# Sparse attention and a mixture of expert attentions: from masked full scores to 256 laid-out keys per query block, with a planned order of all parts

## The chip, the cores and the metric

The kernel runs on one core of a Trainium2 chip. The metric is the device time of one execution in microseconds (us), lower is better. Every time in a profile view is of one execution taken by the hardware profiler.

## The reference

Two stages follow each other, for 4 batches of 768 positions, all in fp32.

```
# stage a: 8 heads of 64, blocks of 32 positions, 24 blocks
scores = scale * q @ k.T
mask = |blk_i - blk_j| <= 1 | blk_i in (0, 23) | blk_j in (0, 23)
mask |= the 3 sampled key blocks of each query block
attn = softmax(where(mask, scores, -1e9)); x = attn @ v      # heads side by side: 512 columns
# stage b: 4 experts of 64, each a causal attention over x
logits = x @ w_gate; the two largest per position, softmax over them -> w
ye = softmax(causal(scale * (x @ wq) @ (x @ wk).T)) @ (x @ wv) @ wo
out = sum of w * ye over the two chosen experts
```

A query of blocks 1 to 22 sees at most 8 key blocks of 32: three of its neighbourhood, the first and the last, and three sampled ones, which may coincide with others. Queries of blocks 0 and 23 see all 768 keys. The weights of queries and keys are scaled so that the experts' scores spread widely, so the maxima are needed.

## The kernel before

**Units.** The work comes in 24 units: per batch four pairs of heads (stage a) and two pairs of experts (stage b). A unit has a first part (operands and maxima, `first_part`, L662) and a second one (`back`, L694: scores, weighted values, denominators).

**Scores.** `scores` (L332) computes transposed scores, keys on partitions and queries in columns, of all 768 keys in stage a and of the causal ones in stage b. Each is the sum of two products of rounded operands (fp32r, L354 and L355): one of the rounded halves, and one of the halves with what the rounding left (`split_hi`, `split_lo`, L250 and L257). The block mask and the negated maxima are further rows of the contraction, so the sum in PSUM is already masked and shifted. ScalarE takes the exponentials (L359, L361).

**Maxima.** Since queries lie in columns there, the maxima come from a second set of score products, queries on partitions, in one rounded product (`maxima_a` L281, `maxima_b` L301), reduced by VectorE (L288, L296, L319) and brought to a row by a transpose and a DMA (`rows_to`, L269).

**Weighted values.** `weighted` (L386) multiplies exponentials and values in full fp32, the two members of a pair in two column tiles of 64 of the PE array (L397, `tile_position=(0, 64 * j)`). The exponentials' sums are added up by GpSimd and VectorE over key tiles (L375, L380), brought across partitions by one-hot products in column tiles of 32 (`denominators`, L413), inverted, and spread over partitions through DRAM (`spread`, L438). `scaled` (L449) splits the result into halves again.

**Experts.** `project_v` (L506) and `load_b` (L562) project x, three rounded products per piece; `project_o` (L591) does the output. They wait for all four pairs of heads of their batch.

**Order.** The parts stand on one line, measured in TensorE's time; some 360 numbers (`PRM`) give their places, and the parts are emitted in that order (L782). Each engine runs its instructions in the order of emission; the semaphores follow from the tiles' uses. Loads go through SP's queue.

Of the kernel before, what the change touches and what calls it, by code (L numbers as in the profile page):

```python
# [16 lines left out]
DRAM = bass.MemoryType.DRAM

# Places of the parts on the line that the order of emission follows; a suffix names the unit.
PRM = dict(  # L20
    LAT=13.1, LAT_a0=12.354, LAT_a1=14.661, LAT_a2=13.384, LAT_b0=17.761, LAT_la0=16.415, LAT_la2=12.42,
    LAT_lb0=13.078, LAT_u=14.078, LAT_v=13.582, LAT_z=24.018, T0=9.302, alag=4.6, alag_a0=4.4, alag_a1=4.0,
    alag_a3=4.708, alag_b1=5.56, alag_la1=4.12, alag_la2=5.967, alag_lb0=8.0, alag_u=4.82, alag_v=5.0,
    alag_w=6.266, alag_y=4.503, alag_z=10.7, c0=1.562, c1=3.8, c2=-0.048, denlag=1.0, denlag_a0=1.581,
    denlag_a1=0.805, denlag_a2=1.457, denlag_a3=0.629, denlag_b0=3.008, denlag_b1=0.834, denlag_f=0.71,
    denlag_la0=0.93, denlag_la1=0.928, denlag_la3=0.912, denlag_lb0=1.946, denlag_u=1.483, denlag_v=0.048,
    denlag_w=1.004, denlag_y=1.221, denlag_z=0.78, fmin=4.924, fmin_a0=1.802, fmin_a1=2.272, fmin_a2=6.216,
    fmin_a3=1.633, fmin_b0=4.822, fmin_b1=4.309, fmin_la1=3.34, fmin_la2=4.016, fmin_la3=4.167,
    fmin_lb0=4.313, fmin_u=4.949, fmin_v=5.643, fmin_w=4.786, fr=0.85, fr_a0=0.7, fr_a1=0.742, fr_a2=0.941,
    fr_b1=0.825, fr_la0=1.085, fr_la1=0.802, fr_v=1.38, fr_y=0.875, fr_z=0.287, glag=0.499, glag_a0=3.123,  # L30
    glag_la0=5.028, glag_v=3.776, half=0, half_a0=1, half_a1=1, half_a2=1, half_b0=0, half_b1=0, half_la0=1,
    half_la1=1, half_la2=0, half_u=1, half_v=0, half_y=1, half_z=1, hi1=0.3, hi1_a1=0.291, hi1_a2=0.053,
    hi1_b0=0.045, hi1_b1=0.224, hi1_f=0.2, hi1_la0=0.481, hi1_la1=0.303, hi1_la2=0.45, hi1_la3=0.409,
    hi1_lb0=0.328, hi1_u=0.332, hi1_v=0.01, ld=2, ld_a0=4, ld_a2=2, ld_b0=3, ld_b1=0, ld_la1=2, ld_lb0=0,
    ld_u=4, ld_w=4, ld_y=2, ld_z=2, lo0=0.132, lo0_a0=0.093, lo0_a1=0.004, lo0_b1=0.001, lo0_f=0.005,
    lo0_la0=0.038, lo0_la1=0.03, lo0_la2=0.136, lo0_la3=0.006, lo0_lb0=0.122, lo0_u=0.117, lo0_v=0.142,
    lo0_w=0.137, lo0_y=0.181, lo0_z=0.194, lo1=0.921, lo1_a0=1.124, lo1_a1=0.807, lo1_a3=0.631,
    lo1_b0=1.141, lo1_b1=0.913, lo1_f=0.497, lo1_la0=0.693, lo1_la1=0.953, lo1_la2=0.039, lo1_la3=1.074,
    lo1_u=0.28, lo1_v=1.246, lo1_y=1.038, lo1_z=0.847, lol=0.366, lol_a1=0.412, lol_a2=0.388, lol_b0=0.371,
    lol_b1=0.332, lol_la0=0.479, lol_la1=0.153, lol_la2=1.504, lol_la3=0.02, lol_u=0.56, lol_v=0.163,  # L40
    lol_w=0.397, lol_y=0.155, lol_z=0.184, mE=3.139, mE_a0=4.355, mE_la0=13.339, mF0=5.0, mF0_a0=6.412,
    mF0_la0=7.098, mQ0=1.448, mQ0_a0=6.073, mQ0_la0=7.051, mQ1=22.409, mQ1_a0=15.958, mQ1_la0=20.473,
    mQ1s=0.807, mQ1s_a0=0.026, mQ1s_la0=1.316, mV=2.0, mV_a0=9.376, mV_la0=8.188, mld=0.0, mld_a0=0.053,
    mld_la0=0.037, mrd=1, mrd_a0=1, mrd_a1=0, mrd_a3=0, mrd_la0=0, mrd_la2=0, mrd_la3=0, mrd_lb0=0, mrd_u=0,
    mrd_v=1, mrd_w=1, mrd_y=1, mrd_z=1, oB=0.794, oB_a0=0.738, oB_a1=0.485, oB_b1=0.351, oB_la0=1.25, pg=1,
    pg_a0=1, pg_a1=2, pg_a3=2, pg_b1=2, pg_f=2, pg_la1=1, pg_la2=2, pg_la3=2, pg_u=2, pg_v=2, pg_y=1,
    pg_z=2, pvs=1.69, pvs_a1=1.676, pvs_b0=1.635, pvs_b1=2.26, pvs_la1=1.8, pvs_la2=1.6, pvs_u=2.865,
    pvs_v=1.971, pvs_z=0.562, ql=-0.014, ql_a0=0.1, ql_a1=-0.0, ql_a3=-0.02, ql_b0=0.027, ql_b1=0.001,
    ql_la0=-0.005, ql_la2=-0.018, ql_la3=-0.04, ql_lb0=0.003, ql_u=-0.023, ql_v=0.011, ql_w=0.012,
    ql_y=-0.032, ql_z=0.02, row0=0.4, rowlag=3.325, rowlag_a0=2.927, rowlag_a2=3.319, rowlag_a3=1.938,  # L50
    rowlag_b0=3.085, rowlag_b1=4.446, rowlag_f=1.273, rowlag_la0=3.327, rowlag_la1=3.362, rowlag_la2=0.687,
    rowlag_lb0=1.967, rowlag_u=1.881, rowlag_v=2.19, rowlag_w=4.275, rowlag_y=2.969, rowlag_z=1.673,
    s1a=0.061, s1a_a1=0.163, s1a_a2=0.003, s1a_a3=0.123, s1a_b0=-0.0, s1a_b1=0.1, s1a_f=0.148, s1a_la1=0.07,
    s1a_la2=0.015, s1a_la3=0.1, s1a_lb0=0.063, s1a_u=0.0, s1a_w=0.204, s1a_y=0.103, s1a_z=0.07, s1b=0.9,
    s1b_a0=0.645, s1b_a1=0.953, s1b_a2=0.971, s1b_b0=0.912, s1b_b1=1.046, s1b_la1=0.951, s1b_lb0=0.904,
    s1b_u=0.86, s1b_v=0.019, s1b_w=0.727, s1b_y=1.0, slot=21.5, slot_a0=37.307, slot_a1=24.896,
    slot_a2=21.953, slot_a3=20.799, slot_b0=8.629, slot_b1=13.986, slot_la0=37.0, slot_la1=21.201,
    slot_la2=21.575, slot_la3=20.0, slot_lb0=18.0, slot_u=10.28, slot_v=6.588, slot_w=26.089, slot_y=25.015,
    slot_z=21.0, slotO=7.453, slotO_a0=8.961, slotO_a1=10.96, slotO_la0=9.856, span0=7.0, subk=1, subk_a0=0,
    subk_a1=1, subk_a2=0, subk_a3=1, subk_b1=0, subk_f=1, subk_la0=0, subk_la1=1, subk_la2=0, subk_la3=0,  # L60
    subk_lb0=0, subk_v=1, subk_w=0, subk_y=0, subk_z=1, subq=1, subq_a0=1, subq_a1=1, subq_a2=0, subq_a3=1,
    subq_b0=1, subq_b1=0, subq_f=1, subq_la1=1, subq_la2=1, subq_la3=1, subq_u=0, subq_v=1, subq_w=0,
    tV=-0.022, tX=7.6, tb0=14.0, tb0L=16.0, tb1=18.397, tb1L=15.332, tf0=3.897, tf1=13.3, tf1L=7.285,
    to=15.0, toL=31.0, tq=1.952, tqL=14.997, vlag=0.747, vlag_a0=0.188, vlag_a1=0.968, vlag_a2=0.558,
    vlag_a3=0.731, vlag_b0=0.703, vlag_b1=1.037, vlag_la0=0.602, vlag_la2=1.208, vlag_la3=1.313,
    vlag_lb0=0.626, vlag_u=0.66, vlag_v=0.168, vlag_w=1.396, vlag_z=0.857, w0=0.007, wsp=55.0, xoff=1.0,
    xoff_a3=2.0, xoff_f=2.37, xoff_la3=0.571,
)
# [9 lines left out]
def block_sparse_then_moe(ctx: ExitStack, tc: tile.TileContext, qT, kT, v, samp, wg, wq, wk, wv, wo, out):  # L78
# [19 lines left out]
    wk2 = ctx.enter_context(tc.tile_pool(name="wk2", bufs=2))
    sm = ctx.enter_context(tc.tile_pool(name="sm", bufs=3))
    ps_st = ctx.enter_context(tc.tile_pool(name="ps_st", bufs=3, space=PSUM))  # L100
    ps_pv = ctx.enter_context(tc.tile_pool(name="ps_pv", bufs=1, space=PSUM))
    ps_s1 = ctx.enter_context(tc.tile_pool(name="ps_s1", bufs=3, space=PSUM))
    dram = ctx.enter_context(tc.tile_pool(name="dram", bufs=3, space=DRAM))
# [5 lines left out]
    NS = 2  # L109
    QA = [ops.tile([128, 2, S], F32R, name=f"QA{i}") for i in range(NS)]  # L110
    QB = [ops.tile([128, 2, S], F32R, name=f"QB{i}") for i in range(NS)]
    KB = [ops.tile([128, 2, S], F32R, name=f"KB{i}") for i in range(NS)]
# [703 lines left out]
```

## Time and profile before

| what | value |
|---|---|
| device time, three runs | 774.3, 776.44, 778.53 us; median 776.44 |
| the profiled execution: first to last instruction (the page gives no time of its own around that span) | 774.1 us |
| DMA moved | 37.45 MB, mean 48 GB/s |
| VectorE, ScalarE, GpSimd busy | 70%, 57%, 50% of the span |
| longest wait group of an engine | ScalarE L359 for TensorE L355, 177.6 us in all |
| SP issues | about 290 DMAs, the record of one 0.3 to 0.6 us |

The page gives for each engine the time in which an instruction of it ran. A matmul's record holds its way through the array too, so two that follow each other overlap in the records; the distance between their starts tells what one costs. "PEld" are the weight loads that go before matmuls. A matmul whose operands are both full fp32 shows as two records. "SPq" rows are DMAs that SyncE issues. The idle time of an engine that is not the bottleneck costs nothing.

### The profile page before, as it was taken

The numbers are of one execution on the slowest core, as the hardware profiler recorded it, in microseconds if no ns is written. First come the engines' busy times: TensorE is split into PE (matmuls) and PEld (weight loads), VectorE is DVE, ScalarE is ACT, GpSimd is POOL, SyncE is SP. The second block draws the span as 40 slices with busy tenths as digits, with TensorE's granted clock in tenths as the row PEclk, the third lists the DMA queues.
The fourth block names the chain that finished last, engine by engine and source line by source line (L and its number), as shares of the span: only waits on it lengthen the run. The fifth ranks groups of instructions, "written<-read, shape, count | busy, mean of one in ns | idle before, by whom it ended". The sixth has DMA issues, their size and how long they took to land.

```text
span 774.1 us, 11317 instructions
## 1 busy us (share of the span) xinstructions
PE 751.7 (97%) x4167; PEld 468.2 (60%) x4167; DVE 540.6 (70%) x878; ACT 441.3 (57%) x731; POOL 385.3 (50%) x325
## 2 busy tenths in 40 slices
PE   4999999999999999999999999999999999999996
PEld 2655555766556556576655655657565655586565
DVE  8887887537878858555778886834776985564634
ACT  8765764374576655428367656644655765535552
POOL 6665853145446935306534892632565655513450
PEclk9999999999999999999999999999999999999999
DMA  7123310102021221100301212120120200010022
...
DMA packets 33904, 37.45 MB, mean 48 GB/s; under 512 B 10428, under 2 KB 23480, under 8 KB 33848
## 3 DMA queue, kind: packets, MB, share of 16 engines
...
q14 instruction: 23, 0.19, 0.1%
...
## 4 chain that ended last, share of the span: by engine, by line
PE 89%; DVE 8%; issue 1%; ACT 1%; DMA 0%; ACTq 0%; DVEq 0%
PE pv L397 28%; PE st L354 13%; PE st L355 10%; PE st L575 9%; PE s L286 7%; PE s L311 5%; PE s L516 5%; PE s L601 4%; PE s L294 3%; PE s L413 3%; PE s L314 2%; DVE mx L288 2%; DVE sum L380 2%; DVE nm L298 1%; DVE u L457 1%
## 5 line engine op out<-in xcount | busy, mean ns | idle before, releaser
L359 ACT ACTIVATE pt<-st 128x512 f32<-128x512 f32 (+1 forms) x256 | 142.9, 582 | 182.3 <-PE st L355 177.6
L397 PE MATMUL pv<-pt,vr 128*64 128x256 f32 (+1 forms) x768 | 191.0, 499 | 0.0
L354 PE MATMUL st<-QA,KA 128*128 128x512 f32 (+4 forms) x512 | 176.8, 357 | 0.0
L355 PE MATMUL st<-QB,KB 128*128 128x256 f32 (+2 forms) x512 | 165.6, 338 | 0.0
L380 POOL TENSOR_TENSOR sum<-sum,pt 128x768 f32<-128x768 f32 (+2 forms) x88 | 141.0, 1604 | 29.8 <-ACT pt L361 25.2
L288 DVE TENSOR_REDUCE mx<-s 128x1 f32<-128x512 f32 x192 | 126.7, 681 | 28.6 <-PE s L286 27.4
L380 DVE TENSOR_TENSOR sum<-sum,pt 128x768 f32<-128x768 f32 (+3 forms) x104 | 101.1, 978 | 48.9 <-ACT pt L361 35.5
L266 POOL TENSOR_TENSOR QB<-qr,QB 64x768 fp32r<-64x768 f32 x32 | 62.5, 1955 | 133.6 <-ACT QB L264 122.8
L354 PEld LDWEIGHTS st<-QA,KA 128*128 128x128 f32 (+1 forms) x512 | 97.4, 190 | 38.1 <-issue 21.8
L397 PEld LDWEIGHTS pv<-pt,vr 128*64 128x64 f32 x768 | 58.6, 136 | 77.0 <-issue 61.6
L355 PEld LDWEIGHTS st<-QB,KB 128*128 128x128 f32 x512 | 97.7, 191 | 9.0 <-issue 1.1
L375 POOL TENSOR_TENSOR sum<-pt 128x768 f32<-128x768 f32 x32 | 61.0, 1917 | 83.3 <-PE s L413 33.2
L319 DVE TENSOR_REDUCE mx<-s 128x1 f32<-128x512 f32 (+3 forms) x128 | 59.5, 501 | 52.5 <-PE s L314 39.1
L361 ACT ACTIVATE pt<-st 128x512 f32<-128x512 f32 x128 | 75.5, 593 | 23.6 <-PE st L355 20.6
L286 PE MATMUL s<-KA,QA 128*128 128x512 f32 x192 | 79.6, 447 | 7.6 <-ACT KA L255 6.3
L366 POOL TENSOR_SCALAR_AFFINE_SELECT pt<-pt 128x128 f32<-128x128 f32 x96 | 36.1, 386 | 89.0 <-ACT pt L359 83.9
L296 DVE TENSOR_REDUCE mx<-s 128x2 f32<-128x512 f32 x96 | 65.5, 682 | 14.6 <-PE s L294 14.3
L397 PE MATMUL pv<-pt,vb 128*64 128x256 f32 (+3 forms) x320 | 62.9, 405 | 0.0
L286 PEld LDWEIGHTS s<-KA,QA 128*128 128x128 f32 x192 | 35.0, 195 | 40.2 <-DVE mx L288 8.5
L311 PE MATMUL s<-KA,QA 64*128 64x512 f32 (+3 forms) x128 | 50.0, 407 | 0.1
L294 PEld LDWEIGHTS s<-KA,QA 128*128 128x128 f32 x192 | 34.0, 196 | 20.8 <-DVE mx L288 11.1
L575 PE MATMUL st<-xh,wqkh 128*128 128x512 f32 (+1 forms) x128 | 45.1, 352 | 0.0
(140 smaller groups left out, 1096.4 us busy)
## 6 DMA issues: line engine op xcount, KB each, us to landing
...
rd<-rc SPq DMA_DIRECT2D x92, 1.5 KB
...
```

Of the source, the lines that this page charges most:

```text
L266: sub.tensor_tensor(dst[64 - o:128 - o, j], x, f(dst)[o:o + 64, j], op=ALU.subtract)
L286: nc.tensor.matmul(s, qa[:, j, r * 128:(r + 1) * 128], ka[:, j, 0:512], start=True, stop=True)
L288: nc.vector.tensor_reduce(mx[:, 0, j, r:r + 1], s, AX.X, op=ALU.max, negate=True)
L296: nc.vector.tensor_reduce(mx[:, 1, j, r - 1:r + 1], s, AX.X, op=ALU.max, negate=True)
L311: nc.tensor.matmul(s[:, o:o + n], qa[0:64, j, r * 128:(r + 1) * 128], ka[0:64, j, k0:k0 + n], start=True, stop=True)
L354: nc.tensor.matmul(s[:, o:o + n], ka[0:hi, j, kc], qa[0:hi, j, q0:q0 + n], start=True, stop=False)
L355: nc.tensor.matmul(s[:, o:o + n], kb_[:, j, kc], qb[:, j, q0:q0 + n], start=False, stop=True)
L359: nc.scalar.activation(p[:, t - t2, q0:q0 + n], s[:, 0:n], AF.Exp, scale=scale)
L361: nc.scalar.activation(p[:, :, q0:q0 + n], s.rearrange("p (a b) -> p a b", a=2), AF.Exp, scale=scale)
L380: eng.tensor_tensor(s_[:, q0:S], s_[:, q0:S], p[:, t - t2, q0:S], op=ALU.add)
L397: nc.tensor.matmul(pv[c][64 * j:64 * j + 64, a - c0:cw], vs(t, j), res["p"][t, j][:, a:a + w], start=t == 0, stop=t == last, tile_position ...
L575: nc.tensor.matmul(s[:, 0:cw], w[:, k, e * 2 * D:(e + 1) * 2 * D], a[:, k, c0:c0 + cw], start=n == 0, stop=n == 3 * KT - 1)
```

## The change

The whole body is new; inputs, outputs and the launch stay.

**Attention.** The unit is now two neighbouring query blocks (64 queries) of all 8 heads: 11 units per batch for blocks 1 to 22, and one for blocks 0 and 23 together (`ends`). GpSimd lays the 256 keys that each block may see side by side (`gather`: 96 of the neighbourhood, 64 of the first and last block, 96 sampled; block numbers in registers). SP loads the values in the same order from DRAM, a DMA for each sampled block (`values`; 7 DMAs per unit, of which 6 have a register address). Scores are full fp32 products of 64 rows by 32 columns, eight tiles of the PE array, queries on partitions; a bf16 product of a one-hot row with a mask row adds the mask for blocks that would count twice. So the maximum is one reduce along the row, the exponential takes it as a bias and returns its sum, and the denominator needs no product. The exponentials are transposed by TensorE (8 per unit), copied out of PSUM by ScalarE or VectorE, and weighted with the values in column tiles of 32 (32 products of 64 columns). x is scaled, transposed and split into rounded halves.

**Experts.** `experts` works on a batch in three chunks of two 128-query tiles, as x becomes ready. Scores (`rows`) are full fp32 products in two row halves of the array (64x128), one expert of a pair in each, over keys 0 to the diagonal; then the same steps: mask by a bf16 product, reduce, exponential with bias and sum, transposes, copies, weighting (128-column weights, 64 moving columns), scaling by gate and denominator, transpose, split, output product and store. The projections are the same three rounded products.

**Buffers.** K and Q of a batch have one buffer each, the laid-out keys and the values three each, x one.

**Order.** `Plan.run` replaces the numbers: each part has an engine, a duration, dependencies, buffers and a due time; a simulation of five engines, eight PSUM banks and buffer slots takes on each engine the ready part with the earliest due time, on TensorE with a preference for staying in the same tiling. The parts are emitted by their planned start. The experts' due times lie about one unit behind the last unit they need.

The core of the diff, after the removal of everything described above:

```diff
-        nc.tensor.matmul(s[:, o:o + n], ka[0:hi, j, kc], qa[0:hi, j, q0:q0 + n], start=True, stop=False)
-        nc.tensor.matmul(s[:, o:o + n], kb_[:, j, kc], qb[:, j, q0:q0 + n], start=False, stop=True)
...
+    def attention(b, u):
...
+        def gather(o):
+            pol.tensor_copy(K[:, :, :, 0:96], win)
...
+            rv = regs(u, ET.Pool)
+            for c in range(2):
+                for k in range(NR):
+                    pol.tensor_copy(K[:, :, c, 160 + 32 * k:192 + 32 * k], KT[:, :, bass.ds(rv[c * NR + k] * 32, 32)])
...
+        def values(o):
+            sp.dma_start(V[0:96, :, 0], bass.AP(tensor=w.tensor, offset=w.offset, ap=[[DM, 96], [32 * DM, 2], [1, DM]]))
...
+            rv = regs(u, ET.SP)
+            for c in range(2):
+                for k in range(NR):
+                    sp.dma_start(V[32 + 32 * k:64 + 32 * k, c, 1], vv[bass.ds(rv[c * NR + k] * 32, 32)])
...
+        def scores(o):
+            for j in range(2):
+                for c in range(4):
+                    for e in range(2):
+                        pe.matmul(Sb[32 * c:32 * c + 32, e, j * 256:(j + 1) * 256], QT[m, 2 * hh + j, q0:q0 + 32],
+                                  KS[ks.i][m, 2 * hh + j, blk], start=True, stop=False,
+                                  tile_position=(64 * e, 32 * c), skip_group_check=True)
...
+                acte.activation(P[p.i][:, e, j], BK[:, bs.i + e, j * 256:(j + 1) * 256], AF.Exp, scale=scale,
+                                bias=MX[mx.i][:, 0, i:i + 1], accum_out=MX[mx.i][:, 1, i:i + 1])
...
+                        pe.transpose(BK[:, bt.i, c:c + 128], P[p.i][:, e, j, h * 128:(h + 1) * 128], ident)
...
+                            pe.matmul(BK[32 * c:32 * c + 32, bo.i, (2 * j + e) * 64:(2 * j + e) * 64 + 64],
+                                      PT[pt.i][:, j, h, 32 * c:32 * c + 32], VS[vs.i][:, blk, h, hd * D:hd * D + D],
+                                      start=h == 0, stop=h == 1, tile_position=(0, 32 * c), skip_group_check=True)
...
+    def rows(b, r, c, vt):
...
+                        pe.matmul(BK[:, banks[e].i + c0 // 512, 0:cw], QE[p][m, r * 128:(r + 1) * 128],
+                                  KE[p][m, c0:c0 + cw], start=True, stop=False, tile_position=(64 * e, 0), skip_group_check=True)
...
+                        pe.matmul(BK[:, bo.i, e * 64:e * 64 + 64], PTE[ptb.i][:, e, t * 128:(t + 1) * 128],
+                                  VB[:, t, (2 * p + e) * D:(2 * p + e + 1) * D], start=t == 0, stop=t == r,
+                                  skip_group_check=True)
...
-    for _, _, fn, args in sorted(line, key=lambda x: x[:2]):
-        fn(*args)
+    order = pl.run()
+    with tc.manual_schedule():
+        for o in order:
+            o.fn(o)
```

More of the change, by code (lines that the diff above doesn't have):

```diff
@@ L15 @@
 AX = mybir.AxisListType
+ET = mybir.EngineType
 PSUM = bass.MemoryType.PSUM
[L17 to L68, printed above, removed]
@@ L69, with __init__ @@
 NEG = float(2.0 ** 33)
 EPS = 1e-9
-def sub_ap(ap, offset, dims):
-    return bass.AP(tensor=ap.tensor, offset=ap.offset + offset, ap=dims)
+MODEL = dict(act=(0.18, 0.00083), actb=(0.31, 0.00083), dve=(0.12, 0.00108), pool=(0.12, 0.0023), sw=0.2,
+             lat=dict(PE=0.4, ACT=0.25, DVE=0.2, POOL=0.25, SP=0.0), dma=2.2, bw=0.22, issue=0.08, keep=6.0, per=9.3)
+class Buf:
+    def __init__(self, pool, vt, n=1):
+        self.pool, self.vt, self.n, self.i, self.users, self.end, self.first = pool, vt, n, None, 0, 0.0, None
@@ L98, in block_sparse_then_moe @@
[L98 to L103, printed above, removed]
+    NT, NB, NR = S // 128, S // 32, samp.shape[1]
+    KT_, EP = DM // 128, E // 2
@@ L105, in f @@
+    U = (NB - 2) // 2
+    WVN = E * D + E
+    scale = 1.0 / float(D) ** 0.5
+    PER = MODEL["per"]
+    sb = ctx.enter_context(tc.tile_pool(name="sb", bufs=1))
+    ps = ctx.enter_context(tc.tile_pool(name="ps", bufs=1, space=PSUM))
     def f(ap):
         return ap.bitcast(F32)
[L109 to L112, printed above, removed]
@@ new lines, in block_sparse_then_moe @@
+    BK = ps.tile([128, 8, 512], F32, name="bk")
+    ident = fixed("ident", [128, 128])
+    tri = fixed("tri", [128, 2, 128], BF)
+    neg = fixed("neg", [128, 64], BF)
+    row = fixed("row", [128, NB, 32], BF)
+    dup = fixed("dup", [128, 160], BF)
+    low = fixed("low", [128, E, E])
+    s32 = fixed("s32", [128, 2 * NR], I32)
+    sreg = fixed("sreg", [1, 2 * NB * NR], I32)
+    sc = fixed("sc", [1, NB * NR], I32)
+    sf = fixed("sf", [128, 8])
+    GS = [[fixed(f"g{n}{i}", [128, 2, E, E] if n < 2 else [128, 2, E]) for n in range(4)] for i in range(2)]
@@ new lines, in block_sparse_then_moe, with evac, dma @@
+    GM = [fixed(f"gm{i}", [128, 2, 2]) for i in range(2)]
+    pl = Plan(pools, 6)
+    op, buf = pl.op, pl.buf
+    vec, pol, acte, pe, sp = nc.vector, nc.gpsimd, nc.scalar, nc.tensor, nc.sync
+    def evac(o, out_, in_):
+        if o.on == "ACT":
+            acte.activation(out_, in_, AF.Copy)
+        else:
+            vec.tensor_copy(out_, in_)
+    def dma(fn, nbytes, n=1, **kw):
+        return op("SP", MODEL["issue"] * n, fn, lat=nbytes / (MODEL["bw"] * 1e6), **kw)
+    src = samp.bitcast(I32)
@@ new lines, in load_samp, with c_ident, c_warm @@
+    def load_samp(o):
+        sp.dma_start(sreg, bass.AP(tensor=src.tensor, offset=src.offset, ap=[[0, 1], [1, 2 * NB * NR]]))
+        for h in range(2):
+            sp.dma_start(s32[64 * h:64 * h + NB], src)
+    c_samp = dma(load_samp, 4000, 3, vt=-100)
+    def c_ident(o):
+        make_identity(nc, ident)
+    o_ident = op("POOL", 0.8, c_ident, vt=-90)
+    def c_warm(o):
+        vec.memset(sf, 0.0)
+        acte.activation(sf[:, 0:1], sf[:, 0:1], AF.Exp)
+    o_warm = op("DVE", 0.2, c_warm, vt=-99)
@@ new lines, in block_sparse_then_moe, with regs @@
+    weights()
+    vals = {}
+    KEEP = 7
+    def regs(u, eng):
+        if (u, eng) in vals:
+            return vals[u, eng]
+        _, x = nc.values_load_multi_w_load_instructions(
+            sc[:, NR * (1 + 2 * u):NR * (3 + 2 * u)], engines=[eng], min_val=0, max_val=NB - 1,
+            skip_runtime_bounds_check_because="block numbers of the sequence")
+        if u < KEEP:
+            vals[u, eng] = x
+        return x
+    kglob, vglob = {}, {}
+    xw, xr, s_use, k_use = {}, {}, {}, {}
@@ new lines, in block_sparse_then_moe @@
+    for b in range(B):
+        loads(b)
+        for u in order_b(b):
+            if u == "g":
+                ends(b)
+            else:
+                attention(b, u)
+        experts(b)
+    order = pl.run()
+    import os
+    if os.environ.get("PLAN"):
+        for o in order:
+            print(f"{o.t:8.2f} {o.dur:5.2f} {o.on:4s} {o.vt:8.2f} {o.name} {o.mode}")
+        for e in ("PE", "ACT", "DVE", "POOL", "SP"):
+            print(e, sum(o.dur for o in order if o.on == e))
+        print("end", max(o.end for o in order))
@@ L787 @@
+    with tc.manual_schedule():
+        for o in order:
+            o.fn(o)
 def kernel(**inputs):
```

1286 lines of the change are left out of this document (679 added, 607 removed).

## The prediction

> **What bounds the kernel now.** I read the page first (engine shares, then the chain that ended last), then the groups by shape on TensorE, then its timeline for true start-to-start times, then the other engines' groups.
>
> ```profile
> span 774.1 us, 11317 instructions
> PE 751.7 (97%) x4167; PEld 468.2 (60%) x4167; DVE 540.6 (70%) x878; ACT 441.3 (57%) x731; POOL 385.3 (50%) x325
> core 0: 774.1 us, clock 0.999
> PE 89%; DVE 8%; issue 1%; ACT 1%; DMA 0%; ACTq 0%; DVEq 0%
> PE pv L397 28%; PE st L354 13%; PE st L355 10%; PE st L575 9%; PE s L286 7%; PE s L311 5%; PE s L516 5%; PE s L601 4%; PE s L294 3%; PE s L413 3%; PE s L314 2%; DVE mx L288 2%; DVE sum L380 2%; DVE nm L298 1%; DVE u L457 1%
> ```
>
> TensorE is busy almost throughout, at the full clock (0.999), and the chain that ended last runs through it for 89%: weighted values (L397), scores (L354, L355), maxima (L286, L294, L311), projections. The three runs lie at 774.3, 776.44 and 778.53 us; the profiled execution's span is 774.1, so I work in spans and add 2.3 us to come to the median.
>
> Every stage is rewritten, so old minus new cannot be done edit by edit. I build TensorE's new work from rates of this trace, check that no other engine has more, and add what TensorE must wait.
>
> **Rates on TensorE.** The duration of a matmul record holds its pipeline latency; what counts is the distance to the next start.
>
> ```profile
> 682.00 8.83 PE s L516 x72
> 156.45 0.28 PE L575 MATMUL st<-xl,wqkh 128*128 128x256 f32 x1
> 156.57 0.28 PE L575 MATMUL st<-xh,wqkl 128*128 128x256 f32 x1
> 746.59 0.39 PE L601 MATMUL s<-woh,oh 128*128 128x512 f32 x1
> 746.82 0.40 PE L601 MATMUL s<-wol,oh 128*128 128x512 f32 x1
> 300.75 0.40 PE L355 MATMUL st<-QB,KB 128*128 128x512 f32 x1
> 301.07 1.07 PE L397 MATMUL pv<-pt,vr 128*64 128x512 f32 x2
> 760.59 1.50 PE L425 MATMUL pv<-rc,qr 128*128 128x128 f32 x12
> 760.36 1.53 PEld L425 LDWEIGHTS pv<-rc,qr 128*128 128x128 f32 x12
> L557 PE MATMUL s<-ident,gr 128*128 128x128 f32 x8 | 1.7, 293 | 0.0
> 681.14 0.86 PE L413 MATMUL s<-sum,onehot 128*32 128x128 f32 x24
> 681.93 0.39 PE L516 MATMUL s<-wvh,xh 128*128 128x260 f32 x1
> 678.44 2.77 PE L397 MATMUL pv<-pt,vb 128*64 128x256 f32 x24
> L516 PEld LDWEIGHTS s<-wvh,xh x96: 186/188/193, 138.0 to 690.2; 128*128 128x128 f32 x96
> ```
>
> - Rounded operands (fp32r): 72 matmuls of 260 columns in 8.83 us, 0.123 each; 256 columns 0.12, 512 columns 0.23.
> - Full fp32: L425's six products are 12 records, so two passes each; a pass over 128 columns takes 1.50 less one latency (0.275) over 11, 0.111 us. Its 12 weight loads of 128 columns also come 0.11 apart. A transpose (L557: 8 records for 8 transposes) is one pass.
> - Column tiles do run side by side: L413's 24 passes of 128 columns in tiles of 32 take 681.14 to 681.93, 0.033 each, less than a third of 0.111. L397's 24 passes in tiles of 64 (16 of 256 columns, 8 of 128; the group's name shows one form) take 678.44 to 681.14, 2.70 us; at 0.11 us per 128 columns, two abreast, they would take 2.2. So tiles reach about 0.8 of their ideal, the change of tiling included.
>
> **The change, on TensorE.** What goes is all of L286 to L413: maxima in a pass of their own, scores split in two products over all 768 keys, sums, denominators. What comes, by those rates:
>
> Attention unit (64 queries, 8 heads; 44 of them). Scores: 16 products of 256 columns, two passes of 0.22 each, in 64x32 tiles, eight abreast: 4 x 0.22, with the masks (16 of at most 160 columns in bf16, priced like fp32r) 1.0 ideal, 1.2 at 0.8. Eight transposes: 0.88. Weighting: 32 products of 64 columns in 32-column tiles, 64 passes, four abreast: ideal 16 x 0.055 = 0.88, at 0.8 1.1; if weights bound it as L413's rate has it, 64 x 0.033 = 2.1. I take 1.4, nearer the stream, since a 32-column load is a quarter of L425's. Two more transposes 0.22. Sum 3.7; 44 make 163 us.
>
> End blocks (4 of them): scores 16 products in 64x64 tiles, 2.6 ideal, 3.2; 24 transposes 2.6; 96 passes of 64 columns two abreast 3.2; 0.2. That is 9.2, 37 in all.
>
> Experts, per batch: V 72 x 0.123 = 8.8; queries and keys 144 x 0.12 = 17.3; scores over 2,688 keys per pair in two row halves abreast, 4.5 ideal, with masks and tile changes 6, twice 12; 84 transposes 9.2; weighting 84 products with 128-column weights and only 64 moving columns, so bound by the loads, 168 x 0.11 = 18.8; 12 transposes 1.3; output 36 x 0.233 = 8.4. Sum 76, 303 in all.
>
> That is 503. Each unit changes tiling about four times and each expert row twice, some 300 changes. A change costs about 0.1: L397's tiles start 0.32 after a matmul of 512 columns (300.75 to 301.07) where 0.23 is usual. I add 30: 533 us.
>
> The trace shows column tiles alone; no 64-row tile stands beside another in it. The bounds of the row tiling are therefore eight abreast as above, and four abreast (the rate of L413), priced as a rival; below eight abreast nothing can be gained.
>
> Loads of weights cost nothing above where a stream hides them: L516 loads for 0.188 us per matmul and still starts one every 0.123. The Trainium skill, page "TensorE: Matmul & The Clock Gate", Part 3 ("The mechanism"), says that a weight load overlaps matmuls in flight only when its row group differs. By that, full tiles would pay load and stream in turn, and the time would be about 1,000 us (worked out as rival 4). L516 disagrees: its loads and streams use the same rows and still overlap.
>
> **What must run beside it.**
>
> ```profile
> L359 ACT ACTIVATE pt<-st 128x512 f32<-128x512 f32 x224 | 129.0, 595 | 161.0 <-PE st L355 156.4 <-DVE mx L288 1.7 <-PE s L286 0.8
> L403 ACT ACTIVATE u<-pv 128x256 f32<-128x256 f32 x24 | 9.1, 379 | 2.3 <-PE pv L397 2.1 <-ACT u L403 0.2
> L288 DVE TENSOR_REDUCE mx<-s 128x1 f32<-128x512 f32 x192 | 126.7, 681 | 28.6 <-PE s L286 27.4
> L319 DVE TENSOR_REDUCE mx<-s 128x1 f32<-128x256 f32 x32 | 12.0, 417 | 8.6 <-PE s L314 8.4
> L541 DVE TENSOR_SCALAR sg<-sg 128x6 f32<-128x6 f32 x4 | 0.7, 172 | 0.1
> L372 POOL COPY sum<-pt 128x128 f32<-128x128 f32 x16 | 4.6, 290 | 2.0 <-POOL pt L366 1.3
> L380 POOL TENSOR_TENSOR sum<-sum,pt 128x768 f32<-128x768 f32 x56 | 106.4, 1904 | 27.9 <-ACT pt L361 25.2
> 1.85 0.59 SPq L133 DMA_DIRECT2D kr<-in_kT_dram  x1
> 2.49 0.60 SPq L134 DMA_DIRECT2D qr<-in_qT_dram  x1
> 0.00:10.00 10.00, 3.27 (x8) 2.19 (x8) 7.54 (x33) 6.68 (x8) 5.35 (x15) 1.00 0.76 196
> 6.30 1.19 PE L286 MATMUL s<-KA,QA 128*128 128x512 f32 x2 [6.30 <-ACT KA L255]
> ```
>
> ScalarE and VectorE: a unit has four exponentials of 256 (0.38 as a copy; with a bias per partition and a running sum, which this trace lacks, up to 0.6; I take 0.5), a copy of 256 (0.38), a reduce over 1,024 (1.2 from 0.417 and 0.681), two operations of 256 (0.42 each), three tiny ones (0.17) and two copies of 512 that either engine may take (0.6): 6.2. The 44 make 273; end blocks about 13 each, 52; experts about 78 per batch by the same rows, 312. Together 637, 320 each if shared: 60% of TensorE's 533, so hidden while units overlap. If every exponential is 0.6 that adds 29, still hidden.
>
> GpSimd lays the keys out: seven copies per unit, six at 0.29 or a little more and one of 768 between 1.0 (one input) and 1.9; 2.7 to 3.7, up to 163 over the kernel, hidden. Its reads of block numbers into registers have no row here.
>
> SyncE: starts of its DMAs lie 0.62 us apart (1.85 to 2.49; record 0.6). A batch issues about 100 (66 with a register address): 62 us of some 140, hidden if a register address costs no more than that. Each values load waits for one of three buffers, and behind it on SP queue the next keys, queries and outputs. Bytes: 0.79 MB of values per unit, about 65 MB in all; the first 10 us moved 196 GB/s at a busy share of 0.76, so 258 at most and 250 us, hidden.
>
> **What TensorE waits.** Today's first matmul starts at 6.3 us. The new one needs the block numbers, 1.6 MB of keys (6.1 us at 258 GB/s, after some seven issues) and a first layout of 4 to 6 us on GpSimd: 15. At the end nothing follows the last expert rows but their chain of exponentials, copies and the output DMA: 10. Keys have one buffer, so at a batch's end the reload waits for its last layout, about 14 us that two or three laid-out units and the experts' rows cover; uncovered it would cost 3 x 14 = 42. For handoffs in the fixed order I take 6% of 533, 30, against 3% idle now; the bounds are 1% and 20% (5 to 107).
>
> Sum: 533 + 15 + 10 + 30 = 588 span, 590 us.
>
> **Rivals.**
> 1. Lighter loads. If narrow streams hide their loads, expert weighting takes 168 x 0.056 (37 less in all) and unit weighting 1.1 (13 less): 540 us. For it: loads of 64 columns in L397 never show as a limit. Against: L425's loads stand 0.11 apart, the length of its stream, and no row shows them closer.
> 2. Row halves in turn. Scores of a unit cost 1.0 more (44), experts' 9 per batch (36), end blocks 2.6 (10): 680 us. Nothing in this trace speaks for or against.
> 3. Slower: SP's queue becomes the bound. An issue with a register address computes it first, and reads of block numbers stand in the same queue. A batch has (776 - 25) / 4 = 188 us before the old time is reached; 34 plain issues take 21, so from 2.5 us per register-addressed issue on, values come late, TensorE stands, and at 2.75 the time is 4 x (21 + 182) + 25, about 835 us. Against: every issue shown here is 0.3 to 0.6.
> 4. Loads and streams in turn. Each full-tile product pays L516's 0.19 for its load on top of its stream: per batch 216 projections 38 more, 84 transposes 16, 168 weighting passes 0.24 for 0.11 (22), 36 outputs 6, together 82; ten transposes per unit 1.9. That is 328 + 84 on the forecast, 1,000 us. Row L516 speaks against it, with 0.123 from start to start. It is the rule of the page named above.
>
> **How the numbers follow.** Forecast 0.57, lighter loads 0.20, row halves 0.12, SP 0.09 (0.01 of it close to the old time), loads in turn 0.02. The range reaches from 530 (rival 1 with few handoff waits) to 690 (row halves, or 20% of handoff waits); it leaves out rivals 3 and 4 and the tails. About 0.5% (3.9 us) is what a measurement of this kernel can tell from no change. Faster: 0.57 + 0.20 + 0.12 = 0.89; same 0.01; slower 0.10.
>
> **What would show it.** TensorE again above 85% busy and most of the chain; scores of a unit in 1.0 to 1.2 us from first start to last (2.2 means rival 2); expert weighting at 0.11 per pass (0.056 means rival 1); SP issues under 1 us; first matmul of scores near 15 us. The forecast is wrong at its root if the chain runs through SP, DMA, GpSimd or ScalarE, or if TensorE is busy under 80%.

## The result and the profile after

| kernel | median of the timed runs, us | lowest to highest | ratio to the kernel before, 95% interval | profiled span, us |
|---|---|---|---|---|
| before | 777.49 | 774.30 to 779.13 | 1 | 774.1 |
| after | 580.78 | 579.83 to 582.55 | 0.7484 [0.7459, 0.7509] | 578.9 |

The change makes the kernel faster by a quarter. The forecast was 590 us. The page of the kernel after, its busy shares and its chain, answers to the first lines shown of the kernel before:

```profile
span 578.9 us, 21208 instructions
...
PE 531.0 (92%) x8496; PEld 438.8 (76%) x8496; DVE 348.0 (60%) x992; ACT 280.1 (48%) x867; POOL 113.0 (20%) x353
...
PE 78%; SPq 9%; DMA 5%; DVE 3%; issue 2%; ACT 2%; ACTq 0%; DVEq 0%
...
DMA packets 50636, 66.40 MB, mean 115 GB/s; under 512 B 17513, under 2 KB 23658, under 8 KB 50538
```

TensorE is still the bound: 531 us busy, 92% of the span, with twice the records (8496 against 4167) in three quarters of the time. New in the chain are SP's queue and the DMAs behind it, 14% together (80 us); 60 us of that are loads of the values, the rest other loads.

**Where the time came from.** I added up the distances from each TensorE start to the next, by line, so that the pipeline latency in the records counts once and a wait counts to the line ahead of it. Before: attention of the heads 434 us, denominators 21, attention of the experts 159, projections 143, other lines about 5. After: attention of the heads 244, attention of the experts 173, projections 146, 563 in all; the first matmul starts at 11.65 and 4.0 us follow the last. The gain lies in the attention of the heads, 190 us, and in the denominators' products, which are gone. The heads now compute 256 keys per query and not 768; and of their 434 us before, 93 were the products for the maxima alone (L286, L294), which are gone too. No run separates the two. The experts, rewritten in the same way, cost about as much as before (14 us more).

The costliest groups of after by shape (mean ns is the length of one record, with its latency; the last column is the idle time of TensorE just before them):

```profile
L864 PE MATMUL bk<-vb,pte 128*128 128x64 f32 x672 | 82.9, 275 | 0.1
L558 PE MATMUL bk<-ks,qt 64*32 64x256 f32 x1408 | 60.4, 407 | 11.6 <-POOL ks L527 11.6
L610 PE MATMUL bk<-vs,pt 128*32 128x64 f32 x2816 | 58.8, 229 | 15.2 <-DMA vs<-in_v_dram 10.5 <-DVE pt L274 1.9 <-issue 1.8
...
L848 PE MATMUL bk<-ident,pe 128*128 128x128 f32 x336 | 49.6, 276 | 6.0 <-ACT pe L832 6.0
L593 PE MATMUL bk<-ident,p 128*128 128x128 f32 x352 | 51.6, 288 | 1.6 <-ACT p L582 1.5
...
L864 PEld LDWEIGHTS bk<-vb,pte 128*128 128x128 f32 x672 | 79.6, 192 | 3.8 <-issue 1.9 <-ACT pte L272 0.3
```

The two longest waits of TensorE are the start (L558, 11.6 us, for the first layout on GpSimd) and the values (L610, 10.5 us, for a DMA). The third is the experts' transposes (L848), 6.0 us, for ScalarE's exponentials.

Three places of TensorE's timeline settle what the trace of before could not show:

```profile
32.49 0.67 PE L558 MATMUL bk<-ks,qt 64*32 64x256 f32 x16
32.95 0.24 PE L566 MATMUL bk<-dup,row 64*32 64x96 bf16 x7
...
303.28 2.89 PE L864 MATMUL bk<-vb,pte 128*128 128x64 f32 x24
...
414.00 0.28 PE L744 MATMUL bk<-xl,wqkh 128*128 128x256 f32 x1
414.11 0.28 PE L744 MATMUL bk<-xh,wqkl 128*128 128x256 f32 x1
414.32 1.10 PE L610 MATMUL bk<-vs,pt 128*32 128x64 f32 x64
415.35 1.35 PE L809 MATMUL bk<-qk 64*128 64x512 f32 x8
```

Sixteen score passes of 256 columns go from 32.49 to 32.95: 0.46 us, where 16 x 0.22 / 8 is 0.44. The eight tiles do run side by side, rows and columns both. A unit's 64 weighting passes go from 414.32 to 415.35: 1.03 us, their stream alone (16 x 0.056 is 0.9). But 24 passes of the expert weighting (128-column weights, 64 moving columns) take 2.89 less one latency of 0.28, 0.113 each, though 64 columns stream in half of that. The step from 414.11 to 414.32 is a change of tiles: 0.21 where a matmul of L744 otherwise takes 0.12, so 0.09 for the change; there are 275 of them.

### The profile page after: what moved, and what is told of

Read it like the earlier page. It is cut to its first block, busy times and chain, and to the rows that moved or that the text cites. A ratio compares the mean times of both kernels' runs of the same rounds, so it can differ in the third digit from the quotient of the medians.

```text
span 578.9 us, 21208 instructions
## 1 busy us (share of the span) xinstructions
PE 531.0 (92%) x8496; PEld 438.8 (76%) x8496; DVE 348.0 (60%) x992; ACT 280.1 (48%) x867; POOL 113.0 (20%) x353
## 4 chain that ended last, share of the span: by engine, by line
PE 78%; SPq 9%; DMA 5%; DVE 3%; issue 2%; ACT 2%; ACTq 0%; DVEq 0%
PE bk L864 13%; PE bk L744 11%; PE bk L809 8%; PE bk L610 7%; PE bk L848 7%; PE bk L906 6%; PE bk L593 6%; PE bk L558 6%; PE bk L724 5%; DMA vs<-in_v_dram 5%; SPq L545 4%; PE bk L696 2%; PE bk L888 2%; PE bk L654 2%; PE bk L467 1%
## 5 line engine op out<-in xcount | busy, mean ns | idle before, releaser
L582 ACT ACTIVATE p<-bk,mx 128x256 f32<-128x256 f32 x176 | 81.4, 475 | 31.7 <-DVE mx L574 21.9
L864 PE MATMUL bk<-vb,pte 128*128 128x64 f32 x672 | 82.9, 275 | 0.1
L864 PEld LDWEIGHTS bk<-vb,pte 128*128 128x128 f32 x672 | 79.6, 192 | 3.8 <-issue 1.9
L827 DVE TENSOR_REDUCE mxe<-bk 128x1 f32<-128x128 f32 (+5 forms) x96 | 55.5, 618 | 38.1 <-PE bk L815 38.1
L832 ACT ACTIVATE pe<-bk,mxe 128x128 f32<-128x128 f32 (+5 forms) x96 | 60.0, 633 | 30.8 <-DVE mxe L827 30.8
L572 DVE TENSOR_REDUCE mx<-bk 128x4 f32<-128x1024 f32 x44 | 53.8, 1222 | 31.8 <-PE bk L566 31.5
L610 PE MATMUL bk<-vs,pt 128*32 128x64 f32 x2816 | 58.8, 229 | 15.2 <-DMA vs<-in_v_dram 10.5
L558 PE MATMUL bk<-ks,qt 64*32 64x256 f32 x1408 | 60.4, 407 | 11.6 <-POOL ks L527 11.6
L610 PEld LDWEIGHTS bk<-vs,pt 128*32 128x32 f32 x2816 | 47.0, 114 | 27.9 <-issue 10.8
L527 POOL COPY ks<-kt 128x128 f32 x264 | 65.5, 296 | 10.6 <-POOL ks L518 8.9
L744 PE MATMUL bk<-xh,wqkh 128*128 128x256 f32 x192 | 55.2, 287 | 0.7 <-DVE qk L274 0.7
L848 PE MATMUL bk<-ident,pe 128*128 128x128 f32 x336 | 49.6, 276 | 6.0 <-ACT pe L832 6.0
L744 PE MATMUL bk<-xl,wqkh 128*128 128x256 f32 x192 | 53.8, 280 | 0.0
L744 PE MATMUL bk<-xh,wqkl 128*128 128x256 f32 x192 | 53.7, 280 | 0.0
L593 PE MATMUL bk<-ident,p 128*128 128x128 f32 x352 | 51.6, 288 | 1.6 <-ACT p L582 1.5
L593 PEld LDWEIGHTS bk<-ident,p 128*128 128x128 f32 x352 | 40.8, 146 | 7.4 <-ACT p L582 3.4
L848 PEld LDWEIGHTS bk<-ident,pe 128*128 128x128 f32 x336 | 38.5, 145 | 8.2 <-ACT pe L832 6.8
L558 PEld LDWEIGHTS bk<-ks,qt 64*32 64x32 f32 x1408 | 24.8, 110 | 22.8 <-POOL ks L527 12.3
```

Source lines behind the costliest of these rows:

```text
L527: pol.tensor_copy(K[:, :, c, 160 + 32 * k:192 + 32 * k], KT[:, :, bass.ds(rv[c * NR + k] * 32, 32)])
L558: pe.matmul(Sb[32 * c:32 * c + 32, e, j * 256:(j + 1) * 256], QT[m, 2 * hh + j, q0:q0 + 32], KS[ks.i][m, 2 * hh + j, blk], start=True, sto ...
L572: vec.tensor_reduce(MX[mx.i][:, 0], BK[:, bs.i:bs.i + 2].rearrange("p e (j k) -> p (e j) k", j=2), AX.X, op=ALU.max, negate=True)
L582: acte.activation(P[p.i][:, e, j], BK[:, bs.i + e, j * 256:(j + 1) * 256], AF.Exp, scale=scale, bias=MX[mx.i][:, 0, i:i + 1], accum_out=MX ...
L593: pe.transpose(BK[:, bt.i, c:c + 128], P[p.i][:, e, j, h * 128:(h + 1) * 128], ident)
L610: pe.matmul(BK[32 * c:32 * c + 32, bo.i, (2 * j + e) * 64:(2 * j + e) * 64 + 64], PT[pt.i][:, j, h, 32 * c:32 * c + 32], VS[vs.i][:, blk, ...
```

## The experiments

Each was timed beside the kernel before and stands as a ratio to it. The last three columns are of the profiled execution; "span less busy" is all the time in which TensorE ran nothing.

| kernel | median, us | ratio [95%] | span | TensorE busy | span less busy | granted clock |
|---|---|---|---|---|---|---|
| after | 580.78 | 0.7484 [0.7459, 0.7509] | 578.9 | 531.0 | 47.9 | 0.976 |
| stream2 | 580.68 | 0.7472 [0.7436, 0.7508] | 578.8 | 528.4 | 50.4 | 0.988 |
| swap | 557.40 | 0.7153 [0.7104, 0.7201] | 557.4 | 503.6 | 53.8 | 0.975 |
| reduce2 | 599.48 | 0.7708 [0.7673, 0.7744] | 598.2 | 531.0 | 67.2 | 0.986 |
| reduce2told | 580.85 | 0.7484 [0.7439, 0.7530] | 579.8 | 526.9 | 52.9 | 0.985 |
| transpose2 | 604.23 | 0.7772 [0.7730, 0.7815] | 602.5 | 559.2 | 43.3 | 0.993 |
| transpose2told | 598.98 | 0.7735 [0.7690, 0.7779] | 598.4 | 556.3 | 42.1 | 0.997 |
| issue55 | 573.35 | 0.7408 [0.7358, 0.7458] | 570.8 | 521.5 | 49.3 | 0.997 |
| keep0 | 580.00 | 0.7475 [0.7426, 0.7523] | 578.9 | 528.1 | 50.8 | 0.984 |
| swap_issue55 | 546.48 | 0.7067 [0.7028, 0.7106] | 543.1 | 494.6 | 48.5 | 0.994 |
| measured | 541.83 | 0.6996 [0.6966, 0.7025] | 539.5 | 495.0 | 44.5 | 0.992 |
| measured_per11 | 540.61 | 0.6969 [0.6934, 0.7005] | 539.5 | 495.1 | 44.4 | 0.992 |

### Loads or streams: stream2 and swap

stream2 lets each expert weighting pass stream 128 columns where 64 are used:

```diff
-  pe.matmul(BK[:, bo.i, e * 64:e * 64 + 64], PTE[ptb.i][:, e, t * 128:(t + 1) * 128],
-            VB[:, t, (2 * p + e) * D:(2 * p + e + 1) * D], ...
+  pe.matmul(BK[:, bo.i, e * 128:e * 128 + 128], PTE[ptb.i][:, e, t * 128:(t + 1) * 128],
+            VB[:, t, 2 * p * D:(2 * p + 2) * D], ...
```

> The weighting of the experts streams 128 columns instead of 64 (the values of both experts of the pair; half of the result is not used), with the same weight loads. Loads bind (the forecast's reason for 18.8 us per batch): each of the 672 passes stays at 0.112 us, the time stays within 3 us of 580.8. Rival, load and stream add up in part: each pass grows by the 0.055 us of 64 columns, 37 us more, about 618.

The time stayed (580.68 against 580.78). In its timeline the same 24 passes:

```profile
303.49 2.94 PE L864 MATMUL bk<-vb,pte 128*128 128x128 f32 x24
```

They take 2.94 where they took 2.89, with twice the columns. So the stream of 64 does not set the length of the pass. That the 128-column load sets it, and not some other cost of every pass, fits a line of after in which as many columns move past narrower weights: the weighting of the end blocks, with 64-column weights in two column tiles:

```profile
37.92 1.62 PE L696 MATMUL bk<-vs,pte 128*64 128x64 f32 x48
```

Its passes start (1.62 - 0.22) / 47, 0.030 us apart, so 0.06 in each tile, near the 0.056 of a stream of 64 columns. The forecast's 0.11 per pass was right, its stated reason fits, and rival 1 (0.056) is wrong here.

swap exchanges the two operands: values become the weights (64 columns), the transposed exponentials stream (128 columns), and the two experts of a pair stand side by side in two column tiles. The result comes out already transposed, so it is the factors that are now spread and transposed (by TensorE, one transpose per pair as before), and a copy each on VectorE and ScalarE are added:

```diff
-  pe.matmul(BK[:, bo.i, e * 64:e * 64 + 64], PTE[ptb.i][:, e, t * 128:(t + 1) * 128],
-            VB[:, t, (2 * p + e) * D:(2 * p + e + 1) * D], ...)
+  pe.matmul(BK[64 * e:64 * e + 64, bo.i, 0:128], VB[:, t, (2 * p + e) * D:(2 * p + e + 1) * D],
+            PTE[ptb.i][:, e, t * 128:(t + 1) * 128], ..., tile_position=(0, 64 * e))
...
+  vec.tensor_copy(OE[oe.i]..., MXE[mx.i][:, 1, 0:2, None].to_broadcast([128, 2, D]))
...
+  acte.activation(OE[oe.i], BK[:, bt.i, 0:128], AF.Copy)
+  vec.tensor_tensor(OE[oe.i], BK[:, bo.i, 0:128], OE[oe.i], op=ALU.mult)
```

> Weighting of the experts with the sides changed: the values (64 columns) are the weights, two experts in two column tiles, the exponentials (128 columns) stream, and the result comes out transposed; the factor per query is spread and transposed instead of the result, which costs one copy on ScalarE and one operation on VectorE more per pair and row. TensorE's sum sets the time and loads bind the old form: 75 us of passes become 38 to 42, 96 more tile changes of 0.1 take 10 back: 549 to 558. Rival, handoffs set it: the longer chain of a row costs as much as it saves, 575 to 590.

It came to 557.40, 23 us less, as expected. First a row of its chain (start, length, count), then the busy shares of its page:

```profile
153.27 1.46 PE bk L864 x24
```

```profile
PE 503.6 (90%) x8496; PEld 400.8 (72%) x8496; DVE 360.2 (65%) x1042; ACT 287.3 (52%) x913; POOL 113.9 (20%) x353
```

24 passes in 1.46 us against 2.82 in the chain of after (303.35 to 306.17), with the same 8496 records in all. L864 falls from 76.2 to 48.9 us, start to start. VectorE and ScalarE rose by 12 and 7 us and stayed beside it. Together the two runs say how to leave the limit of this line, a pass of 0.113 however few columns stream: load the narrower operand. The edit changes two things at once, though, the width of the loads and the two column tiles that it makes room for. Passes of 128 columns 0.061 apart are two tiles at work side by side, each at 0.12, about what a 128-column stream takes (0.111).

### Is the work beside TensorE hidden? reduce2 and reduce2told

VectorE is busy for 60%, and the prediction called its work hidden. reduce2 computes each unit's maxima twice, 44 reduces of 1.22 us, 54 us:

```diff
-  vec.tensor_reduce(MX[mx.i][:, 0], BK[...]..., AX.X, op=ALU.max, negate=True)
+  for _ in range(2):
+      vec.tensor_reduce(MX[mx.i][:, 0], BK[...]..., AX.X, op=ALU.max, negate=True)
```

> The reduce for the maxima of a unit is done twice, 44 x 1.22 = 54 us more on VectorE (60% to 69% busy), nothing more on TensorE. TensorE's sum sets the time: 0 to 6 us more, 581 to 587. Rival, handoffs along a unit's chain set it: the chain of each unit grows by 1.2 us and up to 54 us are added, 610 to 635.

Neither: 18.7 us more. Its page:

```profile
span 598.2 us, 21252 instructions
...
PE 531.0 (89%) x8496; PEld 435.1 (73%) x8496; DVE 396.8 (66%) x1036; ACT 279.4 (47%) x867; POOL 112.7 (19%) x353
...
PE 66%; DVE 21%; SPq 5%; DMA 3%; ACT 2%; issue 2%; ACTq 0%; DVEq 0%
```

TensorE has the same 531.0 us of work and 19 us more of waiting, and VectorE, at only 66%, has 21% of the chain, most of it the doubled line. A second kernel asks whether this is VectorE's room or the order, which was made by a planner that did not know of the second reduce. reduce2told tells it, and changes nothing else:

```diff
-  o_m = op("DVE", dve(1024) + 0.08, maxima, [o_s], vt + 0.2, ...)
+  o_m = op("DVE", 2 * dve(1024) + 0.08, maxima, [o_s], vt + 0.2, ...)
```

> The reduce of a unit twice again, and the planner is told its doubled duration. The doubled reduce alone cost 18.7 us although VectorE was idle for a third of the span. If the cost came from an order laid out for other durations, most of it goes: 581 to 590. Rival, it comes from the longer chain of a unit itself (buffers are held longer, TensorE waits): 595 to 600.

The 18.7 us were gone (580.85).

```profile
PE 526.9 (91%) x8496; PEld 435.4 (75%) x8496; DVE 374.5 (65%) x986; ACT 303.2 (52%) x917; POOL 113.8 (20%) x353
```

Against reduce2, 50 instructions went from VectorE (1036 to 986) to ScalarE (867 to 917): the planner gave copies that either engine may take to the other one, and placed the rest anew. So 54 us of extra work are hidden on an engine with 40% room if the fixed order counts on them, and cost a third of themselves if it doesn't. Whether the moved copies or the new places did it, the run doesn't separate.

### Does TensorE's work enter the time in full? transpose2 and transpose2told

transpose2 does each of the units' transposes twice, 352 more by 0.11, 38 us:

```diff
-  for j in range(2):
+  for j in (0, 1, 0, 1):
       ...
           pe.transpose(BK[:, bt.i, c:c + 128], P[p.i][:, e, j, h * 128:(h + 1) * 128], ident)
```

> The eight transposes of a unit's exponentials are done twice into the same place, 352 more passes of 0.109 us, 38 us more on TensorE and nothing elsewhere. TensorE's sum sets the time: 35 to 40 us more, 616 to 621. Rival, TensorE waits for handoffs anyway: its waits take up most of it, under 600.

23.4 us more, between the two. transpose2told also gives the planner the duration (0.45 to 0.9 for four pairs):

```diff
-  o_t = op("PE", 0.45, tr, ex + [o_ident], vt + 0.4 + 0.1 * e, "full", [bt], [p], ...)
+  o_t = op("PE", 0.9, tr, ex + [o_ident], vt + 0.4 + 0.1 * e, "full", [bt], [p], ...)
```

> The transposes of a unit twice again (38 us more of TensorE's passes), and the planner is told their doubled duration. Untold they cost 23.4 us. If TensorE's sum sets the time, another order can't hide work on TensorE itself, as it did for the reduce on VectorE: 600 to 612. Rival, the waits are the plan's and a better informed plan fills them: under 595.

18.2 us more than after: just under what was expected, and just above the rival's bound. The page of transpose2:

```profile
PE 559.2 (93%) x8848; PEld 470.8 (78%) x8848; DVE 351.9 (58%) x992; ACT 282.5 (47%) x867; POOL 113.8 (19%) x353
...
L610 PE MATMUL bk<-vs,pt 128*32 128x64 f32 x2816 | 55.3, 223 | 5.9 <-DMA vs<-in_v_dram 5.5
```

Busy time rose by 28 and the rest fell by 4.6. L593 grew by 32 us start to start, and L610 shrank by 11; its wait for values fell from 10.5 to 5.5. So when TensorE gets later, part of a wait for DMA is used up, and the time rises by less than the work. A further part may be the granted clock, 0.976 in after and 0.993 here; the next experiment comes back to it.

### The price of an issue: issue55 and keep0

The planner takes 0.08 us for an issue of SP. These are the register-addressed ones of after (shortest, median and longest record in ns):

```profile
L545 SPq DMA_DIRECT2D vs<-in_v_dram x264: 315/316/1726, 22.6 to 511.5; - x132
```

With the register operations between them, the next one of a unit starts 0.53 us later in the median. issue55 corrects this one number; keep0 takes away the planner's preference for staying in the same tiling:

```diff
-  dma=2.2, bw=0.22, issue=0.08, keep=6.0, per=9.3)
+  dma=2.2, bw=0.22, issue=0.55, keep=6.0, per=9.3)     # issue55
+  dma=2.2, bw=0.22, issue=0.08, keep=0.0, per=9.3)     # keep0
```

> The planner is told that SP needs 0.55 us for a DMA instead of 0.08; nothing else is changed. The first values are then issued ahead of the 18 weight loads (they were issued at 19.2 us, behind them). If SP's order costs the start, TensorE's waits in the first 60 us (21 of 60 us not busy) shrink by about 10: 568 to 574. Rival, the bytes bind the start (220 GB/s over the first 30 us) whatever their order: 577 to 583.

> The planner's preference for staying in a tiling of the array is set to 0; the work is the same, the tile changes (275 in the trace of the changed kernel) become more. If a change costs 0.1 us as forecast, the time grows by 0.1 us for each change more, 5 to 20 us if there are 50 to 200 more. Rival, changes are hidden in waits and parts that run in due order shorten the waits: 575 to 582.

keep0 gave 580.00 and moved the number of tile changes only from 275 to 282, so it tests nothing: the due times make the order, not the preference. issue55 gave 573.35, the size that was expected, but not for the reason. The first values are issued at 5.51 and no longer at 19.21, yet TensorE's first 60 us hold no more work than before (38.36 us against 39.07), and the first batch's last x transpose starts at 125.9 against 127.3. The second batch brings most of it: its last x transpose follows 135.4 us later where after takes 140.3. There, SP's queue in after and in issue55:

```profile
182.02 4.36 SPq L545 DMA_DIRECT2D vs<-in_v_dram  x6
186.42 0.41 SPq L535 DMA_DIRECT2D vs<-in_v_dram  x1
186.89 0.91 SPq L540 DMA_DIRECT2D vs<-in_v_dram  x2
188.00 4.10 SPq L545 DMA_DIRECT2D vs<-in_v_dram  x6
```

```profile
180.57 3.77 SPq L545 DMA_DIRECT2D vs<-in_v_dram  x6
184.40 0.41 SPq L535 DMA_DIRECT2D vs<-in_v_dram  x1
184.86 0.92 SPq L540 DMA_DIRECT2D vs<-in_v_dram  x2
185.98 2.94 SPq L545 DMA_DIRECT2D vs<-in_v_dram  x6
```

At a batch's start a unit's value loads are nine issues, one, two and six; later seven. The second group of six ends at 192.1 in after and at 188.9 in issue55; after's first group holds one record of 1.73 us. What TensorE does then in after (in brackets its idle time and what ended it):

```profile
189.78 0.44 PE L467 MATMUL bk<-ident,x 128*128 128x128 f32 x2
191.61 0.32 PE L610 MATMUL bk<-vs,pt 128*32 128x64 f32 x8 [1.40 <-DMA vs<-in_v_dram]
193.37 2.25 PE L610 MATMUL bk<-vs,pt 128*32 128x64 f32 x56 [1.44 <-DMA vs<-in_v_dram]
195.56 1.97 PE L593 MATMUL bk<-ident,p 128*128 128x128 f32 x8
```

And the same stretch by windows (time, then busy us and instructions of PE, PEld, DVE, ACT and POOL, the granted clock, the DMA share, GB/s), first of after, then of issue55:

```profile
190.00:193.50 3.50, 0.66 (x12) 0.32 (x10) 1.11 (x4) 0.38 (x1) 0.00 (x0) 0.91 0.61 134
193.50:197.00 3.50, 3.36 (x63) 2.97 (x63) 0.42 (x1) 0.29 (x1) 0.00 (x0) 0.50 0.70 211
```

```profile
190.00:193.50 3.50, 2.54 (x109) 1.75 (x94) 2.25 (x5) 1.02 (x5) 1.82 (x6) 1.00 0.62 188
193.50:197.00 3.50, 2.43 (x100) 1.71 (x103) 1.82 (x3) 1.71 (x9) 1.81 (x7) 1.00 0.47 138
```

Two waits of 1.4 us for values leave TensorE with 0.66 us of work in 3.5 us. Then the granted clock is 0.50. The chain of after, about 60 us earlier and in this stretch:

```profile
132.00 0.87 PE bk L593 x8
...
138.53 1.03 PE bk L610 x64
...
193.91 1.72 PE bk L610 x54
195.62 1.90 PE bk L593 x8
```

Eight transposes take 1.90 us and not 0.87, 54 weighting passes 1.72 where 64 took 1.03. So the work behind these waits takes twice its time. The Trainium skill, page "TensorE: Matmul & The Clock Gate", Part 1, says that after an idle window of about 3.4 us the clock is halved. The trace agrees in the halving, but TensorE was not idle throughout. The slow stretch lies here, in windows of after:

```profile
189.43:192.84 3.41, 1.11 (x14) 0.50 (x12) 1.55 (x5) 0.67 (x3) 0.00 (x0) 1.00 0.68 150
192.84:199.67 6.83, 6.15 (x113) 4.48 (x113) 1.12 (x2) 0.60 (x1) 0.00 (x0) 0.50 0.80 226
```

It begins while TensorE still waits, lasts 6.8 us, and in the 3.41 us ahead of it TensorE ran for 1.11. The five others between TensorE's first and last matmul follow 3.41 us with 1.4 to 1.9 us of work.

Over the whole span the granted clock is 0.976 in after and 0.997 in issue55. A mean of 0.976 is (1 - 0.976) x 2 x 578.9, 28 us at half clock; 0.997 is 3. And the table above says where the 8.1 us of span went: not into fewer waits (span less busy grew from 47.9 to 49.3) but into busy time, 531.0 to 521.5, with the same 8496 records. That fits the clock: TensorE is busy for 25.4 us of after's half-clock stretches, 12.7 at full clock. But less busy time is not less time.

stream2 and keep0 show only 14 and 19 us at half clock and 3 us less of busy time each, and have as much more of waiting, so that nothing is gained there. The four executions of each kernel say the same: after's, at half clock for 28, 22, 22 and 10 us, have spans of 578.9, 579.1, 580.8 and 578.1; issue55's, with 3, 8, 7 and 14 us, have 570.8, 569.0, 576.4 and 572.3. An execution of issue55 with 14 us of half clock is 5.8 us shorter than one of after with 10, so the clock alone does not make the gain. (In swap's four the span does follow the clock, 557.4 at 0.975 and 551.3 at 0.989.) The gain itself is small: by the ratios it is 5.9 us and not the 7.4 of the medians, and the two intervals only just part, at 0.7458 and 0.7459. How it divides stays open.

### Putting together what helps: swap_issue55, measured, measured_per11

swap_issue55 holds both edits.

> The weighting with sides changed and the planner told of SP's 0.55 us, both. If the two gains lie in different stretches they add: 557 less 10, 544 to 550. Rival, bytes bind the start: 555 to 559.

546.48: swap's 23 and issue55's 7 to 11 add up, as two gains in different stretches should; one is work of TensorE in the experts, the other lies mostly at the batches' starts. measured corrects nine durations of the planner by this case's traces; four of them:

```diff
-  MODEL = dict(..., actb=(0.31, 0.00083), ...)
+  MODEL = dict(..., actb=(0.41, 0.00083), ...)
-  o_m = op("DVE", dve(1024) + 0.08, maxima, ...)
+  o_m = op("DVE", dve(1024) + 0.24, maxima, ...)
-  o_i = op("DVE", 0.2, inv, o_ex, ...)
+  o_i = op("DVE", 0.37, inv, o_ex, ...)
-  pv.append(op("PE", 0.45, weigh, ...
+  pv.append(op("PE", 0.5, weigh, ...
...
```

> On top of swapped weighting and SP's 0.55 us, the planner is told durations from the traces: exponential with sum 0.68 us for 256 columns (0.57 before), the small operations of a unit 0.24 and 0.37, of a row 0.49, the gates 1.6 and 1.0, weighting 0.5 per half unit. The work is the same. If misjudged durations off TensorE cause its waits (about 33 us between its first and last matmul), some of them go: 536 to 543. Rival, what is left is inherent in the chains: 544 to 550.

measured_per11 also changes the distance between the units' due times from 9.3 to 11.0 us (`per`).

> As the run with measured durations, and the distance of due times between units is 11.0 instead of 9.3 (in the traces a batch takes about 135 us for 12 units, 11.3 each). If due times matter only against each other, nothing changes beyond 4 us. Rival, a distance nearer to the true one balances units and expert rows better: 5 us less or more than the run it is compared with.

541.83 and 540.61; the two intervals overlap, and their profiled spans are equal (539.5). measured gains 4.7 on swap_issue55 (0.6996 [0.6966, 0.7025] against 0.7067 [0.7028, 0.7106], so only just clear of the noise), and its gain is in waiting, 48.5 to 44.5:

```profile
PE 495.0 (92%) x8496; PEld 392.9 (73%) x8496; DVE 360.1 (67%) x1040; ACT 287.1 (53%) x915; POOL 115.5 (21%) x353
```

The last two are the fastest kernels of this study, 7% below the changed one and 30% below the old one.

## Why the prediction was right, and where it wasn't

The mechanism was right: TensorE's work plus what it must wait, all other engines beside it. The terms, in us, start to start:

| term | predicted | measured in after |
|---|---|---|
| unit's scores (L558, L566) | 1.2 | 1.35 |
| unit's eight transposes (L593) | 0.88 | 1.16 |
| unit's weighting (L610) | 1.4 | 1.57, of it 0.24 wait for values; undisturbed 1.03 |
| unit's two x transposes (L467) | 0.22 | 0.43 |
| 44 units | 163 | 199 |
| end blocks | 37 | 45 |
| experts and projections | 303 | 319 |
| some 300 tile changes | 30 | 275, inside the rows above |
| gaps inside the rows above | | -32 |
| TensorE's work | 533 | 531 |
| start + end + handoffs | 15 + 10 + 30 | 11.65 + 4.0 + 32.3 |
| span | 588 | 579 |

- **The sum** is right to 2 us in the work and 7 in the waits, and the 2 us are in part luck. The units were priced at 163 and take 199, but 25 us of that are idle time counted to their lines (13.9 behind L610, 6.6 behind L467, 4.3 behind L593), and some 16 are tile changes, if a unit has four of 0.09; the prediction had entered both as lines of their own. The x transposes' 0.43 holds 0.14 of such idle time; undisturbed, a pair takes 0.14 to 0.37, by what stands beside it. Of the units' passes the weighting is furthest off, 1.03 undisturbed against 1.4, some 16 us too much in all; on the other side, the sum had no term for half clock, which is 12.7 of the 531.
- **Expert weighting** not bound by its stream: right (stream2), 0.113 per pass against 0.112 taken; that the loads bind it fits L696. Rival 1 was right for the units (1.03 undisturbed against its 1.1, 1.4 taken) and wrong for the experts, which were 37 of its 50 us.
- **Row halves in turn** (rival 2): refuted by 0.46 us for 16 passes.
- **SP's queue** (rival 3): register-addressed issues start 0.53 us apart in the median (L545, six in 2.9 to 5.6), far from the 2.5 at which it would decide. But SP stands in the chain with 9%, where the prediction had called it hidden. That was the step that failed: 62 us of 140 is an average, and at a batch's change the loads of several units stand behind each other, with TensorE waiting as shown at 190 us. Some 18 of SP's 50 us in the chain lie in the first 20 us, where the first loads are issued.
- **Loads and streams in turn** (rival 4): refuted again, L864 loads for 192 ns each and starts one every 113. (Its 216 projections at 0.19 are 41 per batch and not 38, which lifts its 1,000 by some 12.)
- **ScalarE and VectorE** together 628 us against 637 predicted. The exponential with a running sum is two instructions, 0.475 and 0.206, together above the 0.6 that I had as its bound:

```profile
L582 ACT ACTIVATE p<-bk,mx 128x256 f32<-128x256 f32 x176 | 81.4, 475 | 31.7 <-DVE mx L574 21.9 <-PE bk L593 5.4 <-DVE mx L620 3.3
L582 ACT ACTIVATION_READ_ACCUMULATOR p<-bk,mx 128x1 f32 x176 | 36.3, 206 | 0.0
```

  "Hidden" holds (reduce2told), on the condition that reduce2 shows: the order has to know the duration.
- **The layout on GpSimd**: 113 us, below the bound of 163, hidden but for the first.
- **The clock**: I worked at full clock, as the trace of before had it. After runs at 0.976: the work behind some waits takes twice as long, 25.4 us of busy time where full clock would need 12.7. The sum had no term for it; how much of it reaches the span is not shown.
